# Attention and MLP in one kernel: weights converted in pairs, half of their loads issued by GpSimd, and the first two MLP chunks nested by halves of the hidden features

## The chip, the cores and the metric

The kernel runs on one core of a Trainium2 chip. The metric is the device time of one execution in microseconds (us); lower is better. Times of the kernel before are from three runs; the profile is of one execution. An engine-us is one us of work of one engine.

## The reference

Two parts follow each other. The first is attention for 8 batches and 8 heads of width 64, with 32 global tokens and 512 local ones; local tokens see the global tokens and a window of 32 to each side. The second is an MLP over the 8 x 544 = 4352 rows of the result, with 512 features in and out and 2048 hidden ones.

```python
s_g = scale * q_g @ k_all.T                  # global rows see all 544 keys
out_g = sm(s_g) @ v_all
s_ll = where(abs(i - j) <= 32, scale * q_l @ k_l.T, -1e9)
out_l = sm(concat([scale * q_l @ k_g.T, s_ll])) @ v_all
x = concat([out_g, out_l], axis=2).transpose(0, 2, 1, 3).reshape(B * S, H * D)
h = x @ w_in
out = (0.5 * h * (1 + erf(h / sqrt(2)))) @ w_out
```

`w_in` and `w_out` arrive as 64-bit floats, 8.4 MB each. Everything else is float32.

## The kernel before

**Units and chunks.** Attention goes in 64 units: batch, half of the local rows (256), pair of heads. Four units make the x of one chunk of 256 rows. The MLP goes in 17 chunks: one for each batch and half, and a last one, "g", for the 256 global rows.

**One unit.** k and q are loaded and transposed (`tk`, `tq`), copied out of PSUM (`k1`, `q1`), multiplied (`s`); DVE adds the mask and takes the row minimum or maximum (`m`, then `b`, which scales it), ACT takes the exponential (`e`), DVE normalizes (`n`, `nf`, `ns`), PE transposes (`t`), the result is copied (`ah`), multiplied with v (`o`) and copied into xs (`c`, `x`). `sg`, `sgc`, `sga` collect the scores of the global rows; `gmin` to `gyl` do the global rows' attention once for each batch and four heads. The first eight units (n < NF32 = 8) work in plain float32; the later ones split each operand into a rounded high part and a low remainder and multiply high by high, low by high, high by low.

**MLP.** Chunk rows x are split into xh and xl. The hidden features come in 16 steps f of 128. A step `h` (or its four quarters `hc`) has 12 matmuls of 256 columns (L736-738); after two steps ACT applies gelu (`g`), the result is split (`gh`, `gl`), and `mo` has 6 matmuls of 512 columns per f into acc (L767-769). After 16 f's `ob` copies acc to SBUF and `ow` writes it out.

**Weights.** There are 32 pieces n: even n is step f = n/2 of w_in, odd n of w_out. Each is loaded as raw 32-bit words (512 KB, `w_load`, L179) by SP or ACT into one of seven buffers (pool wa 3, pool wb 4), and converted from 64-bit floats in five instructions: w_1 and w_2 on ACT (L201, L205), w_3 on DVE (L209), w_4 (the rounded part, ACT or DVE), w_5 (the remainder, POOL or DVE). All 32 stay in SBUF afterwards (wi, wo). Chunk 0 goes through f = 0 to 15 at once, so it needs every piece before it ends.

**dm.** `st_dm` (L328) issues transposes of the identity into a PSUM tile that nobody reads, 100 steps of two, wherever PE would be idle. The tile lies in the bank acc1, and the h tiles of the first four f of chunk 0 (HQ = 4) use the banks acc0 and acc1 too; in the list of steps they take "acc", which dm holds until its hundredth step.

**Order.** Nothing is left to chance in the order: each operation is a step with what it needs, the buffers that it takes and frees, its engine or engines, a duration from the table DUR, and a due time worked out from C, AHEAD, OFF and OFF0. A planner at the end of the function (L997-1095) places the steps one by one: the engine that can start earliest starts the step with the earliest due time. The instructions are issued in that order, each engine follows its own part of the list strictly, and waits follow from the data. So a late step holds up whatever stands behind it on its engine. The due times say only which step goes first; they are no times of the chip.

Of the kernel before, what the change touches and what calls it, by code (L numbers as in the profile page):

```python
# [19 lines left out]

# [5 lines left out]

DUR = {
# [5 lines left out]
    "gmin": 0.92, "gex": 0.8, "gn": 0.88, "gt": 0.57, "gah": 0.5, "gal": 0.45, "gagh": 0.25, "gagl": 0.2,  # L48
# [4 lines left out]
}  # L53
# [4 lines left out]
AHEAD = 9.95  # L58

PORT = {"w3", "w4", "w5", "k2", "q1", "k1", "q2", "tgl", "b", "n", "nf", "ns", "vc", "vl", "gvc", "gvl", "xh", "xl", "gh", "gl", "gn"}  # L60
# [25 lines left out]
}  # L86
NDM = 100
NF32 = 8
WLE = "as"
ALAP = 0  # L90
DELTA = {}
LAGS = 3
GX = 0
HQ = 4
NPE = 8
UNP = 100
WB = 10
# [3 lines left out]
def attn_mlp(ctx, tc, q_l, k_l, v_l, q_g, k_g, v_g, w_in, w_out, out):  # L101
# [15 lines left out]
    sm = ctx.enter_context(tc.tile_pool(name="sm", bufs=4))  # L117


    wax, wbx = ExitStack(), ExitStack()  # L120
    wa = wax.enter_context(tc.tile_pool(name="wa", bufs=3, side="right"))
    wb = wbx.enter_context(tc.tile_pool(name="wb", bufs=4))
# [44 lines left out]

    wi = cp.tile([P, NF, 1024], F32R, name="wi")
    wo = cp.tile([P, NF, 1024], F32R, name="wo")
    wraw = {}

    def w_load(e, n):  # L179
        f = n // 2  # L180
        raw = (wb if n in in_b else wa).tile([P, 512, 2], I32, name="wraw", tag="w5")
        wraw[n] = raw
        if n % 2 == 0:
            (nc.sync if e == "s" else nc.scalar).dma_start(
                out=raw.rearrange("p (c x) w -> p c (x w)", c=NCC),
                in_=w_in.bitcast(I32).rearrange("(c p) w -> p c w", p=P)[:, :, f * 256:(f + 1) * 256])
        else:
            (nc.sync if e == "s" else nc.scalar).dma_start(out=raw.rearrange("p x w -> p (x w)"),
                                in_=w_out.bitcast(I32)[f * P:(f + 1) * P, :])

    def early_tiles(e):

        wbx.close()
        late["gp"] = ctx.enter_context(tc.tile_pool(name="gp", bufs=2))
        late["xp"] = ctx.enter_context(tc.tile_pool(name="xp", bufs=1))

    def w_1(e, n):


        x0 = wraw[n].bitcast(U16)[:, :, 1]  # L200
# [27 lines left out]
    for t in a_ts:  # L228
        nc.gpsimd.memset(t, 0.0)
# [917 lines left out]
```

## Time and profile before

| | us |
|---|---|
| median of 3 runs (lowest to highest) | 1062.18 (1061.67 to 1063.47) |
| span of the profiled execution, first to last instruction | 1060.2 |
| PE busy | 1037.8 |
| PE weight loads busy | 933.2 |
| DVE busy | 717.4 |
| ACT busy | 741.7 |
| POOL busy | 361.1 |

The profile gives the profiled execution's time as its span; the median of the runs stands 2.0 us above it. DMA moved 71.28 MB. In a window's row, each engine has its busy time and, in brackets, its count of instructions, followed by the clock granted to TensorE (1.00 is full), the busy share of the DMA engines and the rate of the transfers. In a group's row, the busy time in us and the mean in ns are followed by the engine's idle time just before these instructions and who ended it. In a timeline's row, start and length in us come first, and what stands in brackets is the idle time before it. Two instructions of an engine can overlap by some of their length, so busy time counts overlapped time once, while the sum of means can be larger.

### The profile page before, as it was taken

The numbers are of one execution on the slowest core, as the hardware profiler recorded it, in microseconds if no ns is written. First come the engines' busy times: TensorE is split into PE (matmuls) and PEld (weight loads), VectorE is DVE, ScalarE is ACT, GpSimd is POOL, SyncE is SP. The second block draws the span as 40 slices with busy tenths as digits, with TensorE's granted clock in tenths as the row PEclk, the third lists the DMA queues.
The fourth block names the chain that finished last, engine by engine and source line by source line (L and its number), as shares of the span: only waits on it lengthen the run. The fifth ranks groups of instructions, "written<-read, shape, count | busy, mean of one in ns | idle before, by whom it ended". The sixth has DMA issues, their size and how long they took to land.

```text
span 1060.2 us, 22053 instructions
## 1 busy us (share of the span) xinstructions
PE 1037.8 (98%) x7296; PEld 933.2 (88%) x7296; DVE 717.4 (68%) x2175; ACT 741.7 (70%) x1644; POOL 361.1 (34%) x408
## 2 busy tenths in 40 slices
PE   6879999999999999999999999999999999999998
PEld 5769899999989899899899899998899989999896
DVE  5878867776767777777877777777877777662000
ACT  6849777786768777786769676787769686773231
POOL 4122335234333333334233433334333433243121
PEclk9989999999999999999999999999999999999999
DMA  8655442322322232223222232223222332101000
GB/s 235 172 163 163 124 88 54 75 47 59 72 56 42 54 75 47 63 43 75 52 59 40 58 70 52 58 50 78 42 62 39 62 73 46 47 16 33 1 21 20
DMA packets 273234, 71.28 MB, mean 67 GB/s; under 512 B 258528, under 2 KB 266720, under 8 KB 273120
## 3 DMA queue, kind: packets, MB, share of 16 engines
q1 hardware_dynamic: 270192, 65.03, 27.5%
q10 hardware_dynamic: 2928, 4.85, 1.4%
q8 instruction: 57, 0.93, 0.4%
q14 instruction: 57, 0.47, 0.1%
HBM read 60.88 MB, written 8.91 MB: 66 GB/s over the span
## 4 chain that ended last, share of the span: by engine, by line
PE 94%; DMA 3%; DVE 1%; ACT 1%; issue 0%; SPq 0%; ACTq 0%; DVEq 0%
PE h L736 13%; PE h L738 12%; PE acc L767 12%; PE h L737 12%; PE acc L769 12%; PE acc L768 12%; PE o L559 6%; PE s L449 5%; PE t L523 3%; PE go L687 2%; PE sg L602 2%; PE t L524 1%; DMA wraw<-in_moe_w_out_dram 1%; PE o L572 1%; DMA wraw<-in_moe_w_in_dram 1%; PE gt L647 1%
## 5 line engine op out<-in xcount | busy, mean ns | idle before, releaser
L165 POOL TENSOR_TENSOR gl<-gf,gh 128x512 fp32r<-128x512 f32 x135 | 175.8, 1302 | 457.7 <-DVE gh L160 241.6
L736 PE MATMUL h<-xh,wi 128*128 128x256 f32 x1088 | 315.9, 290 | 0.0
L738 PE MATMUL h<-xh,wi 128*128 128x256 f32 x1088 | 304.3, 280 | 0.0
L737 PE MATMUL h<-xl,wi 128*128 128x256 f32 x1088 | 304.1, 279 | 0.0
L767 PE MATMUL acc<-wo,gh 128*128 128x512 f32 x544 | 219.2, 403 | 0.0
L769 PE MATMUL acc<-wo,gh 128*128 128x512 f32 x544 | 215.0, 395 | 0.0
L768 PE MATMUL acc<-wo,gl 128*128 128x512 f32 x544 | 214.9, 395 | 0.0
L736 PEld LDWEIGHTS h<-xh,wi 128*128 128x128 f32 x1088 | 205.0, 188 | 10.3 <-issue 0.6
L737 PEld LDWEIGHTS h<-xl,wi 128*128 128x128 f32 x1088 | 205.3, 189 | 6.2
L738 PEld LDWEIGHTS h<-xh,wi 128*128 128x128 f32 x1088 | 204.8, 188 | 0.0
L324 ACT ACT_TABLE_LOAD x131 | 168.1, 1283 | 38.9 <-PE h L738 36.9
L324 ACT ACTIVATE gf<-h 128x512 f32<-128x512 f32 x136 | 81.3, 598 | 80.8 <-PE h L738 76.4
L769 PEld LDWEIGHTS acc<-wo,gh 128*128 128x128 f32 x544 | 102.2, 188 | 24.6
L324 ACT ACTIVATE a_t<-a_t,sm 128x192 f32<-128x192 f32 (+1 forms) x256 | 117.0, 459 | 1.4 <-DVE sm L474 0.7
L767 PEld LDWEIGHTS acc<-wo,gh 128*128 128x128 f32 x544 | 102.2, 188 | 13.4 <-issue 0.2
L768 PEld LDWEIGHTS acc<-wo,gl 128*128 128x128 f32 x544 | 102.4, 188 | 13.1 <-POOL gl L165 0.3
L165 POOL TENSOR_TENSOR vs<-vr,vs 128x512 fp32r<-128x512 f32 x56 | 73.0, 1303 | 109.6 <-ACT vs L158 51.5
L468 DVE CUSTOM_DVE_ANT_0 a_t<-s,mask 128x192 f32<-128x192 f32 (+1 forms) x256 | 81.1, 369 | 23.9 <-PE s L449 23.6
L543 DVE TENSOR_TENSOR at<-t,at 128x512 fp32r<-128x512 f32 x112 | 67.8, 620 | 15.9 <-ACT at L158 14.3
L559 PE MATMUL o<-at,vs 128*128 128x256 f32 x448 | 74.5, 288 | 0.1
L158 ACT ACTIVATE at<-t 128x512 fp32r<-128x512 f32 x112 | 59.1, 542 | 21.5 <-PE t L524 11.8
L559 PEld LDWEIGHTS o<-at,vs 128*128 128x128 f32 x448 | 63.0, 188 | 8.2 <-issue 2.1
(123 smaller groups left out, 1659.8 us busy)
## 6 DMA issues: line engine op xcount, KB each, us to landing
raws<-in_v_l_dram SPq DMA_DIRECT2D x64, 128.0 KB, 2.4
out_dram<-ob SPq DMA_DIRECT2D x32, 256.0 KB, 2.1
raws<-in_k_l_dram SPq DMA_DIRECT2D x224, 36.0 KB, 1.9
vr<-in_v_l_dram SPq DMA_DIRECT2D x116, 64.0 KB, 2.1
raws<-in_q_l_dram SPq DMA_DIRECT2D x224, 32.0 KB, 1.9
wraw<-in_moe_w_in_dram SPq DMA_DIRECT2D x12, 512.0 KB, 4.1
wraw<-in_moe_w_out_dram SPq DMA_DIRECT2D x11, 512.0 KB, 4.9
wraw<-in_moe_w_out_dram ACTq DMA_DIRECT2D x5, 512.0 KB, 3.9
```

Source lines behind the costliest of these rows:

```text
L158: nc.scalar.activation(out=out, in_=in_, func=AF.Copy)
L165: (nc.vector if e == "v" else nc.gpsimd).tensor_sub(**kw)
L324: nc.scalar.activation(func=func, **kw)
L468: nc.vector.tensor_tensor_reduce(out=a_t[:, j, aoff[half][i]:aoff[half][i] + w], in0=s[:, c:c + w], in1=masks[half][:, c:c + w], scale=1.0 ...
L543: nc.vector.tensor_sub(out=at[:, 1], in0=st.pop((u, "t", j))[:, :n * P].rearrange("p (n q) -> p n q", q=P), in1=at.bitcast(F32)[:, 0])
L559: nc.tensor.matmul(out=o[:, :, qsl], lhsT=l.rearrange("p s e -> p (s e)"), rhs=r, start=(n == 0), stop=(n == 3), skip_group_check=True)
L736: nc.tensor.matmul(out=h, lhsT=hi, rhs=xh, start=(c == 0 and not (key == (0, 0) and f < HQ and f % 2)), stop=False, skip_group_check=True)
L737: nc.tensor.matmul(out=h, lhsT=hi, rhs=xl, start=False, stop=False, skip_group_check=True)
L738: nc.tensor.matmul(out=h, lhsT=lo, rhs=xh, start=False, stop=(c == NCC - 1), skip_group_check=True)
L767: nc.tensor.matmul(out=acc[t], lhsT=gh[:, f % 2, tsl], rhs=hi, start=(f == 0), stop=False)
L768: nc.tensor.matmul(out=acc[t], lhsT=gl[:, f % 2, tsl], rhs=hi, start=False, stop=False)
L769: nc.tensor.matmul(out=acc[t], lhsT=gh[:, f % 2, tsl], rhs=lo, start=False, stop=(f == NF - 1))
```

## The change

**Pairs.** For f = 0 to 7 the pieces 2f and 2f+1 share one buffer (pool we, four buffers of two pieces), and w_1 to w_5 each run once on both, with 1024 columns. f = 8 to 15 stay single and use pool wa (three buffers). The converted weights lie in two tiles, w0 for f < 8 and w1 for f >= 8; the second is allocated when the first eight units and the pairs are done, in the space of their buffers.

**Issuing engine.** The loads of n < 16 are issued by GpSimd, the others by ACT or SP.

**Nesting.** Chunk 0 is cut into two pieces. The order is chunk 0 with f = 0 to 7, chunk 1 with f = 0 to 15, chunk 0 with f = 8 to 15, then chunks 2 to 15 and g as before. Chunk 0's split x (xx, four tiles of 256 KB) is written to DRAM and read back before its second piece, and so are its two partial sums, to which DVE adds the second piece's (`ml_ea`).

**The first eight units** get buffers of their own (kn, qn, kt0, qt0, vre two each, two more a_t, sm 6 instead of 4), so that more than one can be under way. `sg` writes the global scores directly (one copy instead of a copy and an add), with the queries placed by two small DMAs (`st_tg0`); `o0` writes the two heads to the two halves of the partitions, and `c0` is one copy.

**Others.** dm is gone, and h always uses its own two banks. `b` is gone: the scale -SC is in `m`, which takes the minimum. Due times, durations and order constants are new.

```diff
-    wi = cp.tile([P, NF, 1024], F32R, name="wi")
-    wo = cp.tile([P, NF, 1024], F32R, name="wo")
+    late["w", 0] = cp.tile([P, NF // 2, 2, 1024], F32R, name="w0")
...
-        raw = (wb if n in in_b else wa).tile([P, 512, 2], I32, name="wraw", tag="w5")
-        wraw[n] = raw
+        if n >= NF:
+            wraw[n] = wa.tile([P, 1, 512, 2], I32, name="wraw", tag="w5")
+        elif n % 2 == 0:
+            wraw[n] = we.tile([P, 2, 512, 2], I32, name="wpair", tag="w8")
+        raw = wraw[n][:, 0] if n >= NF else wraw[n - n % 2][:, n % 2]
         if n % 2 == 0:
-            (nc.sync if e == "s" else nc.scalar).dma_start(
+            {"s": nc.sync, "a": nc.scalar, "p": nc.gpsimd}[e].dma_start(
...
-        x0 = wraw[n].bitcast(U16)[:, :, 1]
-        nc.scalar.activation(out=wraw[n][:, :, 0], in_=x0, func=AF.Copy, scale=2.0 ** -13, bias=-0.5 + 2.0 ** -14)
+        x0 = wraw[n].bitcast(U16)[:, :, :, 1]
+        nc.scalar.activation(out=wraw[n][:, :, :, 0], in_=x0, func=AF.Copy, scale=2.0 ** -13, bias=-0.5 + 2.0 ** -14)
...
-                scale=1.0, scalar=-3.0e38, op0=ALU.add, op1=ALU.max,
+                scale=-SC, scalar=3.0e38, op0=ALU.add, op1=ALU.min,
...
-                nc.tensor.matmul(out=o[0:64, j, qsl], lhsT=vr[:, slot, u[2] % 2, j, :], rhs=a[:, n, :],
-                                 start=(n == 0 and j == 0), stop=(n == 3), skip_group_check=True)
+                nc.tensor.matmul(out=o[64 * j:64 * j + 64, qsl], lhsT=st["vr", head(u)][:, slot, u[2] % 2, j, :], rhs=a[:, n, :],
+                                 start=(n == 0), stop=(n == 3), skip_group_check=True)
...
+    def ml_xo(e, key, p):
+        if p == 0:
+            st["xd", key] = dr.tile([NP, P, 2, CH], F32R, name="xd", tag="xd")
+        nc.sync.dma_start(out=st["xd", key][p].bitcast(F32), in_=st["xx", key, p].bitcast(F32))
+
+    def ml_xi(e, key, p):
+        xx_tile(key, p)
+        nc.sync.dma_start(out=st["xx", key, p].bitcast(F32), in_=st["xd", key][p].bitcast(F32))
...
+    def ml_ea(e, key, t):
+        o = st[key, "ob", t]
+        nc.vector.tensor_add(out=o, in0=st[key, "acc"][t], in1=o)
...
+    pieces = [(k, 0, FH) for k in keys[:NEST - 1]] + [(keys[NEST - 1], 0, NF)] + [(k, FH, NF) for k in keys[NEST - 2::-1]] if NEST > 1 else [(keys[0], 0, NF)]
+    pieces += [(k, 0, NF) for k in keys[NEST:]]
...
+        step(("wl", n), w_load, (n,), ("s" if i < 2 else WLE) if n >= PQ else "p", due - 6.0, [], [("we" if pair else "wa", n - n % 2 if pair else n)] if n % 2 == 0 or not pair else [],
+             issues=1, size=0.52, after=("wl", wl[i - 1]) if i else ("lk", units[0]))
...
-    for i in range(NDM):
-        step(("dm", i), st_dm, (i,), "t", 1e4, [("dm", i - 1) if i else ("tk", units[0])], [("acc", "dm")] if not i else [], [("acc", "dm")] if i == NDM - 1 else [])
```

More of the change, by code (lines that the diff above doesn't have):

```diff
@@ L229, in attn_mlp, with a_of, head @@
         nc.gpsimd.memset(t, 0.0)
+    a_ts += [ea.tile([P, 2, AW], F32, name=f"a_e{i}") for i in range(2)]
+    for t in a_ts[2:]:
+        nc.gpsimd.memset(t[:, :, 224:256], 0.0)
+    def a_of(u):
+        return a_ts[u[2] if u in first8 else u[2] % 2]
+    def head(u):
+        return u[0], u[1], u[2] - u[2] % 2
     sgr = [cp.tile([P, R], F32, name=f"sgr{j}") for j in range(2)]
@@ L324, in act @@
         nc.scalar.activation(func=func, **kw)
-    def st_dm(e, i):
-        if i == 0:
-            st["dm"] = ps_o.tile([P, DM], F32, name="dm", tag="acc1")
-        for n in range(2):
-            nc.tensor.transpose(out=st["dm"][:, n * P:n * P + P], in_=ident, identity=ident)
     def st_tk(e, u):
@@ L592, in st_sg @@
         b, half, p = u
-        s = ps_s.tile([P, 512], F32, name="sg", tag="s")
+        early = units.index(u) < NSG
+        s = (ps_o if early else ps_s).tile([P, 512], F32, name="sg", tag="acc0" if early else "s")
         st[u, "sg"] = s
-        whole = (u, "kt") in st
-        for n, kk in enumerate([st[u, "kt"]] if whole else [k1, k2]):
+        for n, kk in enumerate([st[u, "kt"]] if (u, "kt") in st else [k1, k2]):
             if half == 0:
@@ L805, in step @@
+        if name[0] in ("wl", "w1", "w2", "w3", "w4", "w5"):
+            due += WO[name[1]]
         nodes[name] = dict(name=name, fn=fn, args=args, due=due, needs=[x for x in needs if x is not None], after=after,
-                           takes=list(takes), frees=list(frees), size=size, table=table, port=port and name[0] in PORT,
+                           takes=list(takes), frees=list(frees), size=size, issues=issues, table=table, port=port and name[0] in PORT,
                            eng=({k: d[k] for k in eng} if isinstance(d, dict) else
-                                {k: (d if not issues else 0.5 * issues) for k in eng}))
@@ L824, in attn_mlp @@
-    step(("early",), early_tiles, (), "-", 0.0, [("w5", n) for n in in_b])
-    step(("late",), late_tiles, (), "-", 0.0, [("w5", n) for n in wl if n not in in_b])
+        pair = n < NF
+        due = FA - 8.0 + first[n // 2] + (0.0 if n % 2 == 0 or pair else 3 * PW)
+        step(("wl", n), w_load, (n,), ("s" if i < 2 else WLE) if n >= PQ else "p", due - 6.0, [], [("we" if pair else "wa", n - n % 2 if pair else n)] if n % 2 == 0 or not pair else [],
+             issues=1, size=0.52, after=("wl", wl[i - 1]) if i else ("lk", units[0]))
@@ L827, in attn_mlp, with w5 @@
+        step(("w5", m), w_5, (m,), "pv", due, [("w4", m)], frees=[("we" if pair else "wa", m)], dur="w5" + d)
+    step(("early",), early_tiles, (), "-", 0.0, [("w5", n) for n in range(0, NF, 2)] + [(x, u, *y) for u in first8 for x, *y in (("o", 1), ("sg",))])
+    def w5(n):
+        return "w5", n if n >= NF else n - n % 2
+    step(("late",), late_tiles, (), "-", 0.0, [("w5", n) for n in wl if n >= NF])
     for n, u in enumerate(units):
@@ L941, in attn_mlp @@
             step(("xl", key, p), ml_xl, (key, p), "vp", C0 - 29.9 + 0.1 * p, [("xh", key, p)], [], [] if key == "g" else [("xs%d" % p, (*key, p))], early=n < 2)
-        for f in range(NF):
+            if part:
+                step(("xo", key, p), ml_xo, (key, p), "s", C0 - 5.0 + 0.1 * p, [("xl", key, p), ("xo", key, p - 1) if p else None], [], [("xx%d" % p, (key, a))], issues=1, size=0.26)
+        for f in range(a, b):
             hb = [("h", (key, f // 2))] if f % 2 == 0 else []
-            w = [("w5", 2 * f)] if not n else []
-            if not n and f < HQ:
+            new = n == 0 or (f >= FH and n == NEST - 1)
+            w = [w5(2 * f)] if new else []
+            xr = [("xi" if back else "xl", key, c) for c in range(NCC)]
+            if f in (a, b - 1):
@@ L1079, in attn_mlp @@
         if x["size"]:
-            dma = max(dma, t + 0.5) + x["size"] / 0.26
-            end = max(end + 2.2, dma + 0.8)
+            end = t
+            lane = lands[k == "p"]
+            for _ in range(x["issues"]):
+                end = max(end, lane[-8] if len(lane) > 7 else 0.0)
+                dma = max(dma, end + 1.55) + x["size"] / x["issues"] / 0.36
+                end += ISSUE[k]
+                lane.append(max([dma + 0.4] + [z + 0.17 for z in lane[-1:]]))
+            busy[k], end = end, lane[-1]
         got[x["name"]] = end + (0.16 if k == "t" else 0.0)
```

353 lines of the change are left out of this document (209 added, 144 removed), and 30 rows, old and new, of tables (DUR, OFF, OFF0).

## The prediction

> **What bounds the kernel now.** I read the page's head and its 40 slices first, then the windows of the start and of the rest, then the start row by row.
>
> ```profile
> span 1060.2 us, 22053 instructions
> PE   6879999999999999999999999999999999999998
> PEclk9989999999999999999999999999999999999999
> PE 94%; DMA 3%; DVE 1%; ACT 1%; issue 0%; SPq 0%; ACTq 0%; DVEq 0%
> ```
>
> ```profile
> core 0: us, PE busy (x) PEld busy (x) DVE busy (x) ACT busy (x) POOL busy (x), PEclk, DMA share, GB/s
> 0.00:197.68 197.68, 180.58 (x1254) 158.66 (x1255) 147.76 (x416) 142.93 (x326) 63.87 (x89) 0.97 0.52 138
> 0.00:85.20 85.20, 68.10 (x477) 58.10 (x477) 62.48 (x177) 55.84 (x140) 21.25 (x43) 0.94 0.67 186
> 990.00:1020.00 30.00, 30.00 (x195) 26.94 (x194) 1.70 (x4) 8.94 (x17) 6.43 (x5) 1.00 0.05 18
> 85.20:1055.10 969.90, 969.71 (x6822) 875.09 (x6820) 654.94 (x1999) 685.32 (x1505) 339.80 (x365) 1.00 0.26 57
> 5.00:45.00 40.00, 35.91 (x257) 29.85 (x258) 32.04 (x101) 31.49 (x81) 9.26 (x16) 1.00 0.78 218
> 197.68:256.70 59.02, 59.02 (x436) 54.11 (x435) 42.07 (x137) 45.01 (x100) 22.16 (x24) 1.00 0.30 62
> 197.68:1060.20 862.52, 857.23 (x6044) 774.54 (x6042) 569.66 (x1760) 598.78 (x1319) 297.18 (x319) 1.00 0.24 51
> 15.00:40.00 25.00, 24.27 (x188) 19.89 (x185) 23.28 (x76) 23.27 (x66) 5.41 (x5) 1.00 0.83 238
> ```
>
> From 85.2 to 1055.1 us PE is busy 969.71 of 969.90 at full clock. That stretch is the matmul work itself, so nothing that the change does to other engines there is worth time. What can be won lies ahead of it. Chunk 2's first h matmul starts at 197.68, and 862.52 us follow. Before that, PE looks busy for 180.58 us, but part of this is filler:
>
> ```profile
> L332 PE MATMUL dm<-ident x200: 272/273/473, 8.9 to 77.9; 128*128 128x128 f32 x100
> ```
>
> ```profile
> 0.00:85.20 85.20, 28.63 (x200) 24.32 (x200) 0.94 0.67 186
> ```
>
> ```profile
> 46.49 1.25 PE L332 MATMUL dm<-ident 128*128 128x128 f32 x10
> 50.45 3.71 PE L572 MATMUL o<-ao,vr 128*64 128x128 f32 x16 [2.70 <-DVE ao L160]
> 67.35 1.96 PE L572 MATMUL o<-ao,vr 128*64 128x128 f32 x16
> 75.39 1.22 PE L602 MATMUL sg<-kt,gs 128*128 128x256 f32 x2 [3.53 <-DVE sm L468]
> 78.61 0.56 PE L736 MATMUL h<-xh,wi 128*128 128x256 f32 x1
> ...
> 55.29 2.19 DVE L165 TENSOR_TENSOR xl<-xs,xh 128x256 fp32r<-128x256 f32 x3
> ```
>
> The second row is the windows' row for dm alone: 28.63 us of PE time go to transposes whose result nobody reads. The first h of chunk 0 comes at 78.61, right after the last of them (77.9), although its inputs xl were done at 55.29+2.19 = 57.5: chunk 0's first h tiles live in the PSUM bank that dm holds to its end. After PE gaps of 2.70 and 3.53 us the clock is low: the o group takes 3.71 instead of 1.96 (1.75 lost), and the matmuls from 75.39 to 81.3 run at about half rate (some 2.95 lost). So useful PE work before 197.68 is 180.58 - 28.63 - 4.7 = 147.25 us. The other 50 us are what the start loses.
>
> In the same 85.2 us DVE and ACT are busy 62.48 + 55.84 = 118.3 engine-us, 69% of two engines; in 15 to 40 they reach 23.28 and 23.27 of 25, 93%. Later ACT and DVE stand still for weights that SP issued late, behind attention loads:
>
> ```profile
> 47.73 0.67 ACT L201 ACTIVATE wraw<-wraw 128x512 int32<-128x512 uint16 x1 [4.31 <-DMA wraw<-in_moe_w_in_dram]
> ...
> 42.08 1.31 SPq L358 DMA_DIRECT2D raws<-in_k_l_dram  x2
> 43.49 0.53 SPq L184 DMA_DIRECT2D wraw<-in_moe_w_in_dram  x1
> ```
>
> **The change part by part.**
>
> *Nesting, and dm gone.* The MLP needs only half the weights for its first 24 f-steps (chunk 0 with f 0-7, then chunk 1), and h has its own bank from the start. PE work stays: same matmul counts. One f-step is 12 h at 0.118 us apart and 6 acc at 0.233, 2.82 us; 990 to 1020 shows PE full at this pace. A chunk is 45.1 us, and a middle chunk of 59.02 has 13.9 us of attention. Of the 147.25 us, two chunks of MLP are 90.2, units 8-11 13.9, and the first eight units 43.2.
>
> *Pairs.* A weight costs now, over ACT and DVE, (29.14 + 27.21)/20 = 2.82 engine-us:
>
> ```profile
> 0.00:85.20 85.20, 29.14 (x49) 27.21 (x44) 10.34 (x7) 0.94 0.67 186
> ```
>
> ```profile
> L201 ACT ACTIVATE wraw<-wraw 128x512 int32<-128x512 uint16 x20 | 13.5, 675 | 18.9 <-DMA wraw<-in_moe_w_in_dram 14.1 <-DMA wraw<-in_moe_w_out_dram 4.8
> ...
> L158 ACT ACTIVATE vgs<-raws 128x640 fp32r<-128x640 f32 x32 | 23.6, 737 | 9.4 <-PE go L687 8.8 <-DMA raws<-in_v_g_dram 0.2
> L158 ACT ACTIVATE vs<-vr 128x512 fp32r<-128x512 f32 x31 | 19.5, 629 | 4.4 <-PE o L559 3.2 <-DMA vr<-in_v_l_dram 0.8 <-DMA vr<-in_v_g_dram 0.3
> ...
> L543 DVE TENSOR_TENSOR at<-t,at 128x512 fp32r<-128x512 f32 x56 | 38.6, 689 | 8.2 <-ACT at L158 6.7
> L543 DVE TENSOR_TENSOR at<-t,at 128x384 fp32r<-128x384 f32 x56 | 30.8, 550 | 7.7 <-ACT at L158 7.6
> ```
>
> No row has 1024 columns. Bounds: the time of one 512 (675) and of two. From the slopes (ACT 108 ns per 128 columns, DVE 139) a pair costs about 1.06 on ACT and 1.25 on DVE against 1.35 and 1.38: I take 0.28 saved on each of two ACT steps and 0.13 to 0.15 on each of three DVE steps, 0.98 per pair. A pair costs 2x2.82 - 0.98 = 4.66. A POOL subtract is pure streaming and saves nothing.
>
> *Smaller edits of the first units.* st_b goes, sg's two steps become one, c0's two copies one:
>
> ```profile
> L474 DVE TENSOR_SCALAR sm<-sm 128x4 f32<-128x4 f32 x64 | 11.3, 177 | 1.1
> L608 ACT ACTIVATE sgr<-sg 64x256 f32<-64x256 f32 x32 | 12.1, 379 | 1.3
> L615 DVE TENSOR_TENSOR sgr<-sg,sgr 64x256 f32<-64x256 f32 x32 | 13.2, 413 | 4.8 <-ACT sgr L608 4.2
> L158 ACT ACTIVATE xs<-o 64x256 f32<-64x256 f32 x10 | 3.7, 374 | 1.6 <-PE o L572 1.5
> ```
>
> That is 0.18 + 0.4 + 0.37 = 0.95 per unit. The rest of the 118.3, 118.3 - 56.35 = 62, is about 6.5 units (8 had k and q, 7 the exponential, 5 the o), 9.5 each; afterwards 8.5. In later chunks st_b saves DVE time beside a full PE: nothing, as for the new priorities there. The o0 halves in two column groups cost between 1.89 (as now, 16 at 0.118) and half of it if they run side by side; the nearest row is the same matmul in line, so I take no gain and keep 8 x 0.95 = 7.6 us for the range.
>
> *Sum of the start.* Up to the first MLP step: eight units and three pairs, 8 x 8.5 + 3 x 4.66 = 82 engine-us. ACT and DVE have work from about 9 us, where dm now starts behind the first k transposes. Between 69% and 93% I take 85%, 1.7 engine-us per us, because the weights, late by 4.31 us in the row above, now have a queue and eight slots of their own: 9 + 82/1.7 = **57 us**. By then PE has done about 40 of its 43.2. PE then needs 147.25 - 40 = 107.3: chunk 2 at 164.3 at best. ACT and DVE need in the same stretch five pairs (23.3), 16 single weights (45.1), a middle chunk (42.07 + 45.01 = 87.1) and the other chunk's MLP (10.64 x 45.1/30 = 16.0): 171.5/1.7 = 101, 158. So PE is last by 6 us only, and waits will show.
>
> *What is added.* Nesting sends xx (4 x 256 KB) and the partial sums (2 x 256 KB) out and back, 12 DMAs on SP, and one more crossing to each of two pieces.
>
> ```profile
> out_dram<-ob SPq DMA_DIRECT2D x32, 256.0 KB, 2.1
> wraw<-in_moe_w_in_dram SPq DMA_DIRECT2D x12, 512.0 KB, 4.1
> ```
>
> A return waits for the tile that chunk 1 frees, and behind it on SP stand k, q, v loads and half of the late weights; PE waits for it at the crossing unless mo steps cover it. Nothing to 2.1 per crossing each way; I take 2.1 twice, 4.2. dm's cover of the clock is gone: two cold spells as seen, 4.7, bounded by none and one per unit (8 x 2.35 = 18.8). The Trainium skill, "TensorE: Matmul & The Clock Gate", section "Part 4: PE-mode transpose", says that transposes do not count as busy for the gate; by that, dm warmed nothing, its loss costs nothing, and the sum would be 4.7 lower. The trace has clock 1.00 in 5 to 45 with dm in it, which does not decide it.
>
> 164.3 + 4.2 + 4.7 = 173.2 for chunk 2; + 862.5 = 1035.7 of span; the median stands 2.0 above this profile's span: **1037.7 us**, 2.3% faster.
>
> **GpSimd's loads.** Sixteen DMA issues move from SP and ACT to POOL; behind one that waits for a pair's slot stand gl, the subtracts and the edge products, and PE waits for gl. The trace has no POOL issue: between 0.5 (an SP row) and much more, if POOL must share with DVE. That they disturb each other is seen:
>
> ```profile
> L165 DVE TENSOR_TENSOR xl<-xs,xh 128x256 fp32r<-128x256 f32 x47 | 33.7, 741 | 2.0 <-ACT xh L158 1.7
> L165 DVE TENSOR_TENSOR xl<-xg,xh 128x256 fp32r<-128x256 f32 x4 | 1.7, 426 | 36.4 <-ACT xh L158 36.4
> L165 POOL TENSOR_TENSOR gl<-gf,gh 128x512 fp32r<-128x512 f32 x135 | 175.8, 1302 | 457.7 <-DVE gh L160 241.6 <-ACT gh L158 183.9 <-DMA vr<-in_v_l_dram 9.5
> ```
>
> The same subtract takes 741 beside POOL and 426 where POOL is idle. I take one POOL instruction's time, 1.3 us: 16 issues are 21 us of an engine that was busy 9.26 of 40. Hidden.
>
> **Rivals.**
> 1. *ACT and DVE keep their 69%* (1.39 per us): start at 9 + 59 = 68, chunk 2 at 68 + 171.5/1.39 = 191.4, PE's waits hidden in it: 1053.9 + 2.0 = 1056. For it: the chain through one unit is as long as now (PE's 2.70 us for ao, 3.53 for sm), and only more tiles per unit in flight can cover it.
> 2. *POOL's loads starve: slower.* If a load can only be written while DVE is idle (20% in 5 to 45), 1.3 becomes 6.5, the sixteenth is out at 9 + 104 = 113, and the first eight f end near 118.5 instead of 57 + 22.6: 39 later, of which attention of units 8-11 fills about 7. 1037.7 + 32 = 1070. It decides from about 6.0 us a load. Against it: only some DVE instructions would block. The Trainium skill, "SBUF — State Buffer", section "SBUF: two separate sides", states such a trap: DVE's two-port modes keep GpSimd from writing DMA descriptors. No run here shows it for a DMA; the 741 against 426 is the nearest.
> 3. *Cold clock throughout*: 18.8 instead of 4.7, 1052.
> 4. *Given back*: crossings and SP's order eat the gain, 1060 to 1064.
> That the change doesn't do what it says would show as the first h at 78 again; nothing holds it there now.
>
> **Chances.** Forecast (1020 to 1050) 0.56; rival 1 0.15; rival 2 0.13; rival 3 0.11; rival 4 0.05. Low end: 93% gives 9 + 44 = 53, chunk 2 at 160.3 with no waits, 1024.8, and part of o0's 7.6: 1020. High end, with rivals 1 and 3: 1057. Measurement tells 0.2% from no change. Faster 0.56 + 0.15 + 0.11 = 0.82, same 0.05, slower 0.13.
>
> **What would show it.** First h near 57, not 78; PE idle small from there; chunk 2 near 173; 59 us per middle chunk as before; POOL's weight DMAs 1 to 2 us apart and wraw waits on ACT under 1 us each (else rival 2); o0 groups near 1.9 us (3.7 everywhere is rival 3); DVE and ACT at 85% from 10 to 150 (70% is rival 1). A changed middle chunk would overturn the whole account.

## The result, and the profile after

The change is slower by 0.8%: 1071.55 us (1071.21 to 1071.61, four runs) against 1061.93 us (1061.32 to 1063.47, four runs) before, a ratio of 1.0084 with a 95% interval of 1.0072 to 1.0097, so small but clear of the spread of the runs. The forecast was 1037.7 us. The page of the changed kernel, its head and the first line of its chain:

```profile
span 1069.8 us, 21532 instructions
PE 1022.6 (96%) x7096; PEld 911.1 (85%) x7096; DVE 676.1 (63%) x2040; ACT 750.3 (70%) x1653; POOL 367.8 (34%) x427
PE   4887899999999999999999999999999999999998
PEclk9888899999999999999999999999999999999999
PE 82%; DMA 5%; SPq 3%; ACT 3%; DVE 3%; issue 2%; POOL 1%; DVEq 0%; POOLq 0%; ACTq 0%
```

PE was the chain for 94% before and is for 82% now. DMA (3% before), SP's queue (0%), ACT (1%) and DVE (1%) have grown in it, those of DMA and of SP's queue for the most part ahead of chunk 2. In the first 85 us, transfers make 36 us of the chain, SP's issuing of DMAs 28 and PE 5; in the kernel before they make 27, 2 and 28. The windows of the changed kernel, columns as before:

```profile
0.00:25.00 25.00, 11.45 (x52) 8.03 (x53) 8.98 (x32) 10.34 (x26) 11.99 (x38) 1.00 0.88 230
50.00:63.00 13.00, 12.53 (x77) 9.96 (x74) 7.45 (x28) 9.43 (x21) 3.17 (x8) 0.70 1.00 310
63.00:100.00 37.00, 25.77 (x165) 21.03 (x165) 25.66 (x53) 26.82 (x52) 6.41 (x6) 0.82 0.38 103
100.00:150.00 50.00, 45.71 (x299) 41.80 (x298) 38.20 (x83) 34.74 (x66) 12.67 (x9) 0.93 0.57 158
0.00:150.00 150.00, 116.21 (x726) 95.25 (x727) 101.50 (x249) 101.19 (x211) 43.67 (x73) 0.89 0.62 169
215.00:1064.70 849.70, 846.27 (x5954) 763.09 (x5953) 528.12 (x1645) 601.23 (x1327) 299.08 (x327) 1.00 0.24 50
```

From 215 us on PE is busy for 846.27 of 849.70 us at full clock, nearly as before. Ahead of that, up to 150 us, DVE and ACT work 101.50 + 101.19 us of 150, 68% of two engines. From 10 to 150 us, the window that the forecast named, they work 100.46 + 98.64 us, 71%; the forecast had 85%, and the kernel before has 76% there (109.39 + 104.09 us). Chunk 2's first h comes at 203.26 us instead of 197.68, and 173 was forecast (the expectations below name its second matmul, 203.9). From there to the end of the span it is 866.5 us, 4.0 more than the 862.52 before: PE waits 5.4 us in this part (the largest are 2.3 for DVE's `at` and 1.9 for ACT's `gf`), where the kernel before shows no wait. The three longest waits of PE up to 100 us, in its timeline, and two rows between them that are used below:

```profile
22.23 0.71 PE L597 MATMUL sg<-kt,vs 128*64 128x288 f32 x1 [5.25 <-DMA vs<-qgt]
...
23.22 1.70 PE L568 MATMUL o<-ao,vre 128*64 128x128 f32 x13
...
29.84 1.09 PE L568 MATMUL o<-ao,vre 128*64 128x128 f32 x16
...
74.58 0.41 PE L519 MATMUL t<-ident,a_e 128*128 128x128 f32 x2 [4.88 <-DVE a_e L498]
...
88.32 0.69 PE L519 MATMUL t<-ident,a_e 128*128 128x128 f32 x2 [5.32 <-ACT ao L149]
```

Behind the second wait stands a transfer that VectorE waits for (kgr), behind the third ScalarE, which waits for the first single weight, an instruction ahead of the one that PE needs:

```profile
73.23 0.21 DVE L333 STREAM_TRANSPOSE kt<-kgr 128x32 f32<-128x32 f32 x1 [3.62 <-DMA kgr<-in_k_g_dram]
```

```profile
84.46 0.67 ACT L191 ACTIVATE wraw<-wraw 128x512 int32<-128x512 uint16 x1 [5.83 <-DMA wraw<-in_moe_w_in_dram]
```

The chain of waits from 10 to 30 us (start, length, what) and the first issues of GpSimd show where it begins:

```profile
10.69 0.52 SPq L421
11.21 0.04 issue
11.25 10.85 DMA vs<-qgt
```

```profile
7.43 0.92 POOL L174 DMA_DIRECT2D wpair<-in_moe_w_in_dram  x1
8.35 0.56 POOL L178 DMA_DIRECT2D wpair<-in_moe_w_out_dram  x1
8.89 0.75 POOL L174 DMA_DIRECT2D wpair<-in_moe_w_in_dram  x1
```

An issue costs GpSimd 0.55 to 0.92 us. Seven loads of 512 KB go out between 7.43 and 12.7 us, two at 28.5 and 29.7, and seven more between 46.2 and 53.6, because GpSimd had stood in between behind its own waits. In both stretches of seven the DMA engines are full (shares of 1.09 and 1.07 in windows shown below), and SP's 32 KB transfer of qgt needs 10.85 us. The second and the third wait come about in another way. The transfers of kgr take 1.7 us to land (the median) and the first single weight takes 4.26, but SP issues them late. Its issues go out one behind the other, and beside the second seven loads they take longer themselves:

```profile
50.77 2.79 SPq L295 DMA_DIRECT2D vre<-in_v_l_dram  x2
...
55.95 3.33 SPq L306 DMA_DIRECT2D vre<-in_v_l_dram  x2
59.32 4.09 SPq L306 DMA_DIRECT2D vre<-in_v_g_dram  x2
...
80.18 0.42 SPq L174 DMA_DIRECT2D wraw<-in_moe_w_in_dram  x1
```

These three rows of two issues take 10.2 us; in a kernel below with few bytes in flight (e10) the same three take 0.94, 1.99 and 0.90. From 63.4 to 80.2 us SP then issues without a pause, about 0.45 us for each small transfer, and the load for which ACT waits stands at the end of that row.

### The profile page after: what moved, and what is told of

Read it like the earlier page. It is cut to its first block, busy times and chain, and to the rows that moved or that the text cites. A ratio compares the mean times of both kernels' runs of the same rounds, so it can differ in the third digit from the quotient of the medians.

```text
span 1069.8 us, 21532 instructions
## 1 busy us (share of the span) xinstructions
PE 1022.6 (96%) x7096; PEld 911.1 (85%) x7096; DVE 676.1 (63%) x2040; ACT 750.3 (70%) x1653; POOL 367.8 (34%) x427
## 4 chain that ended last, share of the span: by engine, by line
PE 82%; DMA 5%; SPq 3%; ACT 3%; DVE 3%; issue 2%; POOL 1%; DVEq 0%; POOLq 0%; ACTq 0%
PE h L747 11%; PE acc L779 11%; PE h L748 11%; PE h L749 11%; PE acc L780 11%; PE acc L781 11%; PE o L555 5%; PE s L448 4%; PE t L519 2%; PE go L689 2%; PE sg L599 1%; DMA vre<-in_v_l_dram 1%; PE t L520 1%; ACT L323 1%; DMA vs<-qgt 1%
## 5 line engine op out<-in xcount | busy, mean ns | idle before, releaser
L747 PE MATMUL h<-xx,w 128*128 128x256 f32 x1088 | 318.4, 293 | 4.3 <-ACT gf L323 4.3
L748 PE MATMUL h<-xx,w 128*128 128x256 f32 x1088 | 306.3, 282 | 0.4 <-POOL xx L156 0.4
L749 PE MATMUL h<-xx,w 128*128 128x256 f32 x1088 | 306.2, 281 | 0.4 <-DVE w L156 0.4
L779 PE MATMUL acc<-w,gh 128*128 128x512 f32 x544 | 220.5, 405 | 1.9 <-ACT gf L323 1.9
L747 PEld LDWEIGHTS h<-xx,w 128*128 128x128 f32 x1088 | 207.0, 190 | 14.6 <-ACT gf L323 4.7
L780 PE MATMUL acc<-w,gl 128*128 128x512 f32 x544 | 215.3, 396 | 0.0
L781 PE MATMUL acc<-w,gh 128*128 128x512 f32 x544 | 214.8, 395 | 0.0
L748 PEld LDWEIGHTS h<-xx,w 128*128 128x128 f32 x1088 | 207.7, 191 | 5.6 <-POOL xx L156 0.6
L749 PEld LDWEIGHTS h<-xx,w 128*128 128x128 f32 x1088 | 206.9, 190 | 0.6 <-DVE w L156 0.6
L781 PEld LDWEIGHTS acc<-w,gh 128*128 128x128 f32 x544 | 103.0, 189 | 23.6
L149 ACT ACTIVATE gh<-gf 128x512 fp32r<-128x512 f32 x108 | 68.3, 632 | 75.2 <-PE acc L781 73.9
L779 PEld LDWEIGHTS acc<-w,gh 128*128 128x128 f32 x544 | 103.5, 190 | 16.2 <-ACT gf L323 2.0
L780 PEld LDWEIGHTS acc<-w,gl 128*128 128x128 f32 x544 | 103.6, 190 | 12.0
L323 ACT ACTIVATE a_t<-a_t,sm 128x192 f32<-128x192 f32 x240 | 109.5, 458 | 2.7 <-DVE sm L467 2.1
L467 DVE CUSTOM_DVE_ANT_0 a_t<-s,mask 128x192 f32<-128x192 f32 x240 | 76.2, 369 | 46.5 <-PE s L448 46.5
L539 DVE TENSOR_TENSOR at<-t,at 128x512 fp32r<-128x512 f32 (+1 forms) x112 | 68.0, 619 | 46.8 <-ACT at L149 46.5
```

Of the source, the lines that this page charges most:

```text
L149: nc.scalar.activation(out=out, in_=in_, func=AF.Copy)
L323: nc.scalar.activation(func=func, **kw)
L467: nc.vector.tensor_tensor_reduce(out=a_t[:, j, aoff[half][i]:aoff[half][i] + w], in0=s[:, c:c + w], in1=masks[half][:, c:c + w], scale=-SC ...
L539: nc.vector.tensor_sub(out=at[:, 1], in0=st.pop((u, "t", j))[:, :n * P].rearrange("p (n q) -> p n q", q=P), in1=at.bitcast(F32)[:, 0])
L747: nc.tensor.matmul(out=h, lhsT=hi, rhs=xh, start=(c == 0), stop=False, skip_group_check=True)
L748: nc.tensor.matmul(out=h, lhsT=hi, rhs=xl, start=False, stop=False, skip_group_check=True)
```

## The experiments

All but three of these kernels keep the changed kernel's plan, so each engine's order stays as it was but for the edit; in e3, e4 and e5 the planner placed everything anew, so their differences also hold what another order brings. Times are compared with 1071.55 us. The ratio, with its 95% interval, stands against the kernel before. Where the intervals of two kernels overlap, as those of e1, e2, e11, e13 and e23 do with the change's 1.0072 to 1.0097, a difference of 1 to 3 us is not clear of noise.

**What the first transfer costs (e1).**

```diff
-            nc.sync.dma_start(out=gs0[...], in_=qgt[64 * j:64 * j + 64])
+            nc.scalar.activation(out=gs0[...], in_=qgt[64 * j:64 * j + 64], func=AF.Copy)
```

> The order of every engine is that of the changed kernel; only the two 32 KB transfers that place qgt for the first global scores (10.85 us to land, 5.25 us of TensorE waiting) become two ScalarE copies into a tile of their own. Theory A (transfers that land late hold up the first eight units, and each such wait adds to the time): the first global scores start near 17 us in place of 22.2 us, chunk 2 starts 4 to 5 us earlier than its 203.9 us, time 1066 to 1068 us against 1071.55 us. Rival (the waits behind it are fixed by other late transfers, so the gain is used up at the next one, vre at 63 us): chunk 2 within 1.5 us of 203.9 us, time 1070 to 1072 us.

1070.39 us, ratio 1.0075 (1.006 to 1.009). The rival's time holds: the 5.25 us wait went, chunk 2's first h came 1.5 us earlier (201.78), the end 1.2 us earlier, and in its place PE waited 9.0 us for kn, 5.8 for qn and 6.2 for an exponential up to 205 us (2.2, 3.0 and 2.1 in the change).

**Whose queue (e2).** The sixteen loads are issued by ACT instead of GpSimd.

```diff
-            {"s": nc.sync, "a": nc.scalar, "p": nc.gpsimd}[e].dma_start(
+            {"s": nc.sync, "a": nc.scalar, "p": nc.scalar}[e].dma_start(
```

> The sixteen weight loads that GpSimd issues are issued by ScalarE at the same places of the same plan; all other orders are those of the changed kernel. Theory B (what costs the time is GpSimd's own queue, which moves its packets ahead of SyncE's small ones): vre lands in 5 us or less after its issue, vs<-qgt in 5 us or less, time 1062 to 1067 us. Theory C (it is the 3.5 MB as such, in flight in the first 25 us and again from 46 us): the landings stay at 9 to 12 us and the time at 1069 to 1074 us, a few tenths more for sixteen issues on ScalarE.

1069.19 us, ratio 1.0062 (1.0047 to 1.0077). It tells the two less well apart than meant: qgt landed in 2.2 us, but ACT reaches its issues later in its own order (the third load at 12.7 us, the fifth at 19.3), so fewer bytes were in flight then, and the first pair was converted from 21.6 us on instead of 15.1. Its time is 2.4 us lower.

**The bytes (e10).**

```diff
+        z = 64 if e == "p" else 1024
-                out=raw.rearrange("p (c x) w -> p c (x w)", c=NCC), ...[:, :, f * 256:(f + 1) * 256])
+                out=raw.rearrange("p (c x) w -> p c (x w)", c=NCC)[:, :, :z // 4], ...[:, :, f * 256:f * 256 + z // 4])
```

> The sixteen loads of GpSimd keep their places but each brings 32 KB in place of 512 KB; the rest of the four pair buffers is filled once with a constant, so the first eight weight pairs are not the reference's. Theory A/C (bytes in flight make SyncE's transfers late): every small transfer lands in 5 us or less, the 5 us waits of TensorE for vs<-qgt and vre go, chunk 2 starts at 190 to 197 us, time 1058 to 1065 us. Rival (the pace of the first units and of the first MLP pieces is set by the engines' order and work, not by transfers): chunk 2 after 200 us, time 1068 to 1072 us. The filling costs DVE about 4 us at the start, which can hide 1 or 2 us of a gain.

1055.81 us, ratio 0.9934 (0.9918 to 0.9951): 15.7 us less than the change, more than the 6.5 to 13.5 expected and the largest difference of any single edit. The list of DMA issues (KB each, median us to landing), first of the change, then of e10:

```profile
vs<-qgt SPq DMA_DIRECT2D x2, 32.0 KB, 9.9
```

```profile
vs<-qgt SPq DMA_DIRECT2D x2, 32.0 KB, 2.5
```

And the windows from 10 us and from 50 us, of the change and of e10:

```profile
10.00:25.00 15.00, 6.94 (x36) 5.24 (x35) 7.94 (x29) 7.80 (x22) 2.56 (x6) 1.00 1.09 308
50.00:60.00 10.00, 9.53 (x57) 7.75 (x56) 5.72 (x19) 6.59 (x19) 3.17 (x8) 0.61 1.07 352
```

```profile
10.00:25.00 15.00, 12.07 (x66) 8.59 (x65) 9.99 (x32) 11.68 (x30) 3.29 (x7) 1.00 0.50 108
50.00:60.00 10.00, 9.92 (x88) 8.01 (x83) 8.72 (x21) 9.89 (x22) 1.63 (x1) 1.00 0.26 51
```

With the DMA engines half empty, ACT does 11.68 us of work from 10 to 25 us instead of 7.80, and 9.89 instead of 6.59 from 50 to 60. So it is the bytes in flight that make SP's transfers late, and with them DVE and ACT idle. That the pairs themselves arrive sooner is not what is gained: in the changed kernel neither ACT nor DVE waits for a pair's load (no such row among their waits up to 85 us). SP's queue ran ahead too: the load of the first single weight goes out at 66.47 us instead of 80.18, and chunk 2's first h comes at 187.87.

**No load by GpSimd (e5), two pair buffers (e3), no nesting (e4).**

```diff
-PQ = 16
+PQ = 0
```

> No load is issued by GpSimd: SyncE and ScalarE issue all of them, and the plan is worked out anew with that (so orders differ everywhere). If GpSimd's queue is the cost (theory B) this gives 1058 to 1066 us; if the nesting, the lost clock and the pace of the conversions are the cost, 1069 to 1076 us, with chunk 2 still after 200 us.

```diff
-    we = ex.enter_context(tc.tile_pool(name="we", bufs=4))
+    we = ex.enter_context(tc.tile_pool(name="we", bufs=2))
```

> Two buffers for weight pairs in place of four, so at most four 512 KB loads run ahead of the conversions; the plan is worked out anew with that. Theory A/C (the early bursts of 3.5 MB make SyncE's small transfers late): DMA share under 1.0 in 10 to 25 and 50 to 60 us, vre lands in 6 us or less, time 1058 to 1067 us. Rival (loads that come later hold up the conversions, which are the pace): 1071 to 1078 us.

```diff
-NEST = 2
+NEST = 1
```

> No nesting by halves: chunk 0 runs all sixteen feature steps, then chunk 1; weights in pairs and GpSimd's loads stay, the plan is worked out anew. If the nesting brings what the prediction took (TensorE has work for chunk 1 while the second half of the weights is converted): slower than the change, 1075 to 1090 us. If the nesting is what costs (two more transfers of xx and partial sums each way, the order of ScalarE around them): 1058 to 1068 us.

1079.23 us (1.0158, 1.0143 to 1.0173), 1073.90 us (1.0109, 1.0086 to 1.0132) and 1075.46 us (1.0117, 1.0101 to 1.0133). Issuing by SP and ACT alone, and running chunk 0 at one go, are both slower than the change, by 7.7 and 3.9 us. So neither shows GpSimd's issuing or the nesting as the cost; since the planner placed all steps anew, with the due times that came with the change, they do not rule it out either. On the same plan, e2 puts GpSimd as the issuer at some 2.4 us; for the nesting there is no such run. Two pair buffers cut the first burst (DMA share 0.71 from 0 to 25 us instead of 0.88) but the third pair was then converted at 43.9 us only, instead of 29.5.

**The clock (e11, e23).** Transposes of the identity, and small products with a zero operand, just ahead of the steps at which PE waits:

```diff
+    WARM = {("t", (0, 0, 0), 0): 10, ("sg", (0, 0, 0)): 50, ...}
+    ZERO = {("t", (0, 1, 3), 1): 14, ("h", (0, 1), 6): 22}
     for t, i, x in order:
+        if x["name"] in WARM:
+            warm(WARM[x["name"]])
```

> The changed kernel with idle TensorE work put just ahead of seven steps at which it waits (72 transposes of the identity before t, sg and qp of the first units, 20 small products with a zero operand, which add nothing, before two later waits); every other order is unchanged. Theory D (the time lost over the forecast is mainly matmuls at half clock, since nothing keeps the clock up in the waits): the granted clock of 25 to 100 us rises from 0.70 to 0.88 to 0.95 or more, chunk 2 starts 6 to 12 us earlier than 203.9 us, time 1059 to 1066 us. Rival (in these stretches TensorE waits for transfers, ScalarE and VectorE anyway, so faster matmuls only wait longer): clock as high, time 1069 to 1073 us.

> As the warm version, but with 143 transposes and 36 zero products, sized so that they fill the waits at the pace that they showed there (0.117 us each), where 72 and 20 had left 3.55 and 7.41 us of waiting after which the clock was half again. Theory D (the cold matmuls lie on the path to the end): the granted clock of 25 to 100 us is 0.95 or more, time 1055 to 1064 us. Rival (they lie beside waits for transfers and conversions): the clock is as high and the time is 1069 to 1074 us.

1073.26 us (1.0092, 1.0073 to 1.0112) with 72 transposes, which filled the waits only in part, and 1071.72 us (1.0092, 1.0076 to 1.0109) with 143. The second has the clock up from 50 to 150 us. Its windows and PE's timeline:

```profile
63.00:100.00 37.00, 30.88 (x246) 26.52 (x243) 24.20 (x52) 26.63 (x51) 5.91 (x6) 1.00 0.41 108
100.00:150.00 50.00, 48.71 (x339) 44.23 (x338) 39.41 (x82) 34.28 (x65) 12.41 (x9) 1.00 0.55 158
```

```profile
16.88 6.13 PE L330 MATMUL dm<-ident 128*128 128x128 f32 x50
22.94 0.46 PE L607 MATMUL sg<-kt,vs 128*64 128x288 f32 x1
...
23.48 0.93 PE L578 MATMUL o<-ao,vre 128*64 128x128 f32 x13
```

The o matmuls behind the transposes take 0.93 us for 13, against 1.70 us for the same 13 in the changed kernel. ACT and DVE do no more from 63 to 100 us (26.63 and 24.20 of 37) than without (26.82 and 25.66), and the time is the same: the cold matmuls lie beside waits of others. From 25 to 50 us the clock was still 0.86 in e23, so the exclusion is for 50 to 150 us above all.

**Three edits at once (e13).** The edits of e1, e2 and e11 in one kernel.

> Three edits together on the unchanged plan: qgt placed by two ScalarE copies, the sixteen loads issued by ScalarE, the idle TensorE work of the warm version. If the gains of the single edits (1.2 and 2.4 us, and that of the warm version) add up, 1071.5 less their sum; if they are paid out of the same waits, no better than the best of them alone by 1 us.

1071.46 us (1.0092, 1.0062 to 1.0122): the small differences of e1 and e2 did not add, and neither of them is left.

**What the end follows.** Put side by side, the profiles give the start of the last weight conversion (L191 or its line in that kernel, on ACT) and the span:

| kernel | last conversion, us | span, us | difference |
|---|---|---|---|
| change | 141.66 | 1069.8 | 928.1 |
| e1, qgt copies | 139.93 | 1068.7 | 928.8 |
| e2, loads by ACT | 139.13 | 1067.0 | 927.9 |
| e10, few bytes | 126.33 | 1055.8 | 929.5 |
| e11, e23, warm | 141.68, 140.61 | 1071.4, 1069.9 | 929.7, 929.3 |
| e17, less work | 133.45 | 1063.9 | 930.5 |
| e14, five buffers | 138.54 | 1065.3 | 926.8 |
| e22, last version | 128.34 | 1056.5 | 928.2 |

Some 928 us follow the last conversion, whatever was edited; the other kernels on this plan lie between 926.8 and 931.0. This marks where the start ends, but does not show that the weights are its cause: in a fixed order, other events stand as firmly. Chunk 2's first h comes 866.5, 866.9, 867.9 and 866.1 us before the end in the change, e1, e10 and e22. What the weights wait for is the next question. For the sixteen single weights of the change, the groups and the waits of ACT, and the waits of SP from 84 to 143 us, read:

```profile
L191 ACT ACTIVATE wraw<-wraw 128x512 int32<-128x512 uint16 x16 | 10.8, 675 | 17.0 <-DMA wraw<-in_moe_w_in_dram 9.2 <-DMA wraw<-in_moe_w_out_dram 7.8
...
L191 ACT ACTIVATE wpair<-wpair 128x1024 int32<-128x1024 uint16 x8 | 9.1, 1142 | 0.0
```

```profile
SPq L178 <- DVE gsm L638: 9.8, 1, 9.8
SPq L178 <- DVE w L156: 9.5, 4, 5.3
SPq L174 <- DVE w L156: 8.8, 3, 5.2
```

ACT waits 17.0 us for single loads, 5.83 of them for the first. SP waits 18.3 us for DVE to free one of the three buffers (w, the last subtraction) before it can issue the next. The first row, 9.8 us ahead of the fourth load, is probably the same wait under another name: that load went out at 95.55 us, and DVE's subtraction of the first single weight ended at 95.52 (94.16 + 1.36).

**The ring of the single weights (e14), and with few bytes (e16).** Two more raw buffers, which lie where the last pair's converted weights go later, and loads issued up to two places earlier:

```diff
-        late["w", 1] = w2.tile([P, NF // 2, 2, 1024], F32R, name="w1")
+        late["w", 1] = w2.tile([P, NF // 2 - 1, 2, 1024], F32R, name="w1")
+        late["xw"] = xwx.enter_context(tc.tile_pool(name="xw", bufs=2))
-            wraw[n] = wa.tile([P, 1, 512, 2], I32, name="wraw", tag="w5")
+            wraw[n] = (late["xw"] if k in (3, 4, 8, 9) else wa).tile([P, 1, 512, 2], I32, name="wraw", tag="w5")
```

> The plan of the changed kernel, but the single weights have five raw buffers in place of three for their first ten (the two more lie where the last pair of weights is written later), and their loads are issued up to two places earlier. Theory E (the end follows the last weight conversion, 141.7 us, by 928 us, and that conversion is late by the loads: ScalarE waits 17.0 us for wraw in the sixteen single loads, each of which SyncE may issue only when VectorE has freed a buffer): those waits fall under 6 us, the last conversion starts at 128 to 135 us, time 1058 to 1066 us. Rival (the conversions are then held by ScalarE's and VectorE's own work between them): the last conversion after 138 us, time 1068 to 1072 us.

> Both terms together: the first sixteen loads bring 32 KB each (the first eight weight pairs are not the reference's) and the single weights have five raw buffers. If the bytes in the first 60 us and the ring of the single loads are two terms of their own, 1055.8 less what the five buffers bring by themselves: 1043 to 1050 us. If they are the same wait, 1053 to 1056 us.

e14: 1068.60 us (1.0056, 1.0039 to 1.0073), 3.0 us less than the change, against 6 to 14 expected; its rival, that the work in between then holds the conversions, fits (the last one after 138 us). ACT's wait for these loads fell to 5.9 us from 60 to 150 us, all of it for the first load, but the last conversion came only 3.1 us earlier: ACT now waits for other things in between, 6.1 us of it for DVE's steps of the conversions. e16: 1052.50 us (0.9909, 0.9885 to 0.9934), 3.3 us less than e10 and 19.1 less than the change. It lies between the two times expected (up to 1050 if the terms add, from 1053 if they are the same wait), and its interval overlaps that of e10. So the second term is small, and whether it adds to the first is not decided.

**All three at once (e15).** e14 with the edits of e1 and e2.

> The five buffers, qgt placed by two ScalarE copies and the sixteen GpSimd loads issued by ScalarE, on the plan of the changed kernel. If the gains add (the one of the five buffers and up to 3 us of the other two), 1055 to 1063 us; the last conversion plus 928 to 931 us gives the span.

1068.65 us (1.0053, 1.0032 to 1.0074), no better than e14 alone, against 1055 to 1063 expected if the differences added.

**Is it the work (e17)?** The first three conversion steps on an eighth of the columns.

```diff
-        x0 = wraw[n].bitcast(U16)[:, :, :, 1]
+        x0 = wraw[n].bitcast(U16)[:, :, 0:64, 1]
```

> The first three conversion steps (two on ScalarE, one on VectorE) work on an eighth of each weight, so the weights are not the reference's; loads, waits and orders are unchanged. It takes away some 14 us of ScalarE and 8 us of VectorE from the eight pairs and some 18 and 10 us from the sixteen singles. Theory F (what is left of the miss is the pace of ScalarE and VectorE, as the sum of the prediction has it, only at a lower rate): at 1.4 engine-us done per us, 1071.5 falls by some 30 us, to 1036 to 1050 us. Rival (the conversions wait for loads and for VectorE to free buffers, so work taken away turns into waiting): ScalarE's wait for wraw rises above 20 us, time 1060 to 1070 us.

1065.59 us (1.003, 1.002 to 1.0041). By the page's busy times it took 25.4 us off ACT (750.3 to 724.9) and 11.4 off DVE (676.1 to 664.7), less than its expectation said, since a short instruction still takes 0.25 to 0.41 us. At the forecast's 1.7 engine-us per us, 36.8 would be worth 22 us; it brought 6.0, as its rival said (1060 to 1070 us). The groups of ACT up to 204 us show the rest:

```profile
L191 ACT ACTIVATE wraw<-wraw 128x64 int32<-128x64 uint16 x16 | 4.2, 260 | 21.7 <-DMA wraw<-in_moe_w_in_dram 12.3 <-DMA wraw<-in_moe_w_out_dram 9.3
```

The wait for the loads grew from 17.0 to 21.7 us. Work taken away became waiting.

**Bursts (e19), and a version that wins (e20, e21, e22).** GpSimd fills a scratch tile between its loads, so that the loads go out further apart:

```diff
+        for i in range({1: 8, 2: 8, 3: 8, 4: 8, 5: 8}.get(n, 6 if 9 <= n < 15 else 0)):
+            nc.gpsimd.memset(junk, 0.0)
```

> GpSimd fills a small scratch tile 8 times (about 2.4 us) after each of the loads 1 to 5 and 6 times after each of the loads 9 to 14, so that the two bursts of 3.5 MB come over about 17 and 14 us in place of 5 and 7; bytes, queue and plan are those of the changed kernel. If it is the burst that makes SyncE's transfers late: vs<-qgt and vre land in 6 us or less and the time is 1060 to 1067 us. If it is the bytes, or the later landing of the weights costs as much: 1069 to 1075 us.

> The spread loads and the five raw buffers of the single weights together. If the spreading gains as expected of it and the five buffers bring their 3 us: 1057 to 1064 us, at or under the kernel before; if the spreading brings nothing, 1066 to 1072 us.

e19: 1067.09 us (1.0043, 1.0028 to 1.0058), 4.5 us less; qgt lands in 4.7 us, though the DMA share from 10 to 25 us is still 1.02. e20, with e14's buffers: 1063.14 us (1.0001, 0.9991 to 1.0011), 8.4 us less than the change and equal to the kernel before. e21, built on e20, fills 6 times everywhere and takes e1's copies; e22 also moves the first three single loads ahead on SP:

```diff
+        if x["name"] == ("lg", 1):
+            x["fn"](x["on"], *x["args"])
+            for k in range(3):
+                w_load(loads[k]["on"], singles[k])
-    slots = {0: (0,), 1: (1,), 2: (2,), 3: (3, 4, 5), ...}
+    slots = {3: (3, 4, 5), ...}
```

> Spread loads (6 fillings of the scratch tile after each, about 2.1 us), five raw buffers and qgt placed by two ScalarE copies. If the first burst was spread a little too far before (ScalarE waited 4.9 us for three pair loads) and the copies keep their 1.2 us: 1059 to 1062 us; if these trade places with the late small transfers again, 1063 to 1066 us. The last weight conversion plus 927 to 931 us gives the span.

> The same with the first three single weights loaded right behind the global rows of batch 1 on SyncE, about 6 us earlier. If the last conversion still follows the loads, it starts 2 to 4 us earlier and the time is 1056 to 1060 us, under the kernel before; if the other engines' work between the singles now sets their pace, the same as without within 1 us.

e21: 1061.81 us (0.9999, 0.9986 to 1.0011). e22: 1057.72 us (1055.92 to 1062.56, twelve runs), ratio 0.9957 (0.9944 to 0.9971), faster than both kernels, with every weight loaded and converted. Moving the three loads out of SP's row of issues brought 4.1 us against e21, more than e14's two buffers. The wait for the first single load, 5.83 us in the change, is gone, and the singles start at 75.8 us instead of 84.5. The last conversions on ACT, in the timelines of the kernel before, the change and e22:

```profile
124.35 0.67 ACT L201 ACTIVATE wraw<-wraw 128x512 int32<-128x512 uint16 x1 [0.85 <-DVE ao L160]
```

```profile
141.66 0.67 ACT L191 ACTIVATE wraw<-wraw 128x512 int32<-128x512 uint16 x1 [2.07 <-DMA wraw<-in_moe_w_out_dram]
```

```profile
128.34 0.68 ACT L203 ACTIVATE wraw<-wraw 128x512 int32<-128x512 uint16 x1 [1.74 <-DMA wraw<-in_moe_w_out_dram]
```

The change converts its last weight 17.3 us later than the kernel before, although its conversions cost less. What it wins behind that point, 928.1 us to the end against 935.9, is less than half of that.

## Why the prediction was wrong

**The step that failed** is the rate: "Between 69% and 93% I take 85%, 1.7 engine-us per us, because the weights, late by 4.31 us in the row above, now have a queue and eight slots of their own". A queue of its own was read as room of its own. The transfers share the DMA engines, which the row quoted there for 15 to 40 us already had at 0.83. The eight slots let 3.5 MB go out at once into that, twice; the small transfers on which the first eight units depend landed late or were issued late, and DVE and ACT reached 71% from 10 to 150 us, less than the 76% of the kernel before. The Trainium skill, "DMA: Bandwidth & Descriptors", section "Issuing engines are not separate DMA queues", says just this: whichever engine starts them, transfers run on the same 16 DMA engines, and issuing from several saves only issue time. The runs agree: 2.4 us for another issuing engine, 15.7 for the bytes.

A lower rate alone does not mend the sum. At 69%, rival 1 has chunk 2 at 191.4 us, and 203.26 was measured; and 36.8 engine-us less work brought 6.0 us (e17). The start was taken as work divided by a rate, and it is a chain of waits: for transfers, for SP's issues and for buffers.

Point by point:

- *PE bounds from 85 us on, so the gain lies ahead of chunk 2*: right for the kernel before; in the change PE is full only from 215 us on. Of the 33.9 us that the forecast missed, 30.1 lie ahead of chunk 2 (203.26 against 173.2) and 4.0 behind it (866.5 against the 862.5 that were taken over); the median stands 1.75 us above the span instead of 2.0. "PE is last by 6 us only" did not hold: up to 150 us PE is busy for 116.21 us, and weights were converted until 142.
- *First h of chunk 0 near 57*: it came earlier (the first parts from 31 us, two of four by 35; PE's f = 1 from 58). So the kernel is slower although this sign came out better than forecast: it said nothing of the later weights.
- *Pairs save 0.98 engine-us each*: right in size. 1.14 and 1.13 us on ACT and 1.22 on DVE for the first three steps, against twice 0.675, 0.663 and 0.701, is 0.6 of it; on DVE the copy (0.69 against twice 0.50) and the subtraction (1.38 against twice 0.80) bring 0.5 more by these means, some of which hold stretched instructions. GpSimd's subtraction, taken to save nothing, took 2.41 us for a pair against 1.31 for 512 columns. What engine time taken off the conversions is worth, e17 shows: 6.0 us for 36.8.
- *GpSimd's issue, 1.3 us, hidden*: the issue costs 0.55 to 0.92 us, and no wait of PE for `gl` shows. The loads' cost was of another kind, which the sum did not have.
- *Cold clock, 4.7*: the clock was low for longer than taken (0.70 to 0.93 from 50 to 150 us), but keeping it up brought nothing (e23). The time that dm filled had other waits behind it, so its 28.63 us were no reserve.
- *The wait at the crossings, 4.2*: too much; up to 205 us no wait of PE for a returned tile over 0.4 us shows in the change.
- *o0, no gain taken*: wrong the other way. 16 matmuls take 1.09 us at full clock instead of 1.96, near the lower of the two bounds (half of 1.89), so the halves run side by side.
- *Rival 2 (1070)* gave the right time for the wrong reason: its price, 6.5 us for a load, did not occur. *Rival 1*, the 69%, describes the rate that DVE and ACT had, and the forecast named 70% from 10 to 150 us as its sign; but its sum gave 1056. That e10 came to 1055.81 is chance, since its DVE and ACT work some 75% up to 150 us.

Of the 33.9 us between forecast and result, e16 gives back 19.1 (bytes 15.7, ring about 3). So the bytes in flight are shown as the largest single cost in the start. That they alone make the change slower than the kernel before is not shown as strictly: that kernel loads the same bytes, with a DMA share of 0.94 from 10 to 25 us, while e10 goes without most of those of the first sixteen loads. But e20 and e22 load them all and come level with it and below it. The other 14.8 us are not settled. e17 speaks against the amount of conversion work and e23 against the clock. What is left are the waits of DVE and ACT on each other and on PE, and SP's row of issues, in an order with new due times, which no run took apart; e22's three earlier loads (4.1 us) are the only test of that order. Nor is it shown how much of the 15.7 us a better timing could get back: e22 keeps all bytes and gets 13.8 us of the 33.9, by spacing, two buffers, the copies of qgt and earlier loads together.

## What to carry to other kernels

Before giving loads a queue of their own, look at the DMA share of the stretch in which they will run, and at what else is issued there. Where it is near full, as here at 0.83, prefetched bytes can push aside the small transfers that the critical chain needs; here spacing the loads brought 4.5 us. The share alone does not show this: it was 1.02 with spaced loads too. Look also at the queue that issues the small transfers: a load behind a row of issues is late however fast it lands. Where filler fills an engine's waits, removing it frees nothing until the wait's own cause is found, as the 28.63 us showed. A fixed distance from an event to the end tells where the start ends, not what makes it late; that took runs which change one thing each.

## What the runs showed of the hardware

- A 32 KB transfer landed in 2.2 to 2.5 us where few bytes were in flight, in 4.7 with spaced loads, and in 9.9 behind seven loads of 512 KB, with the DMA share at 1.09.
- Beside such loads, SP's issues themselves took longer: 2.79 to 4.09 us for two, against 0.90 to 1.99 for the same ones in e10.
- Float32 transposes of the identity did keep the clock up: after 50 of them the 13 o matmuls took 0.93 us instead of 1.70. The column of granted clock reads 1.00 up to 25 us in both kernels, so there the durations are the sign and not the column. The Trainium skill, "TensorE: Matmul & The Clock Gate", section "Part 4: PE-mode transpose", says that transposes do not count as busy in the same way; for these the measurement differs. Whether these ran in the mode that the page means, no run shows.
- Two matmul streams in different column halves overlap: 16 in 1.09 us, against 1.96 before.
